# Transposing k unnormalised in the first attention, with its factors in the exps, and a new schedule for the weight rounding

## The chip, the cores and the metric

One core of a Trainium2 chip. The metric is device microseconds of one execution, checked against the reference. Engines by the names of the profile: PE does the matmuls (TensorE), DVE is VectorE, ACT ScalarE, POOL GpSimd; SP is the sync engine, in whose queue (SPq) all transfers are issued. PEclk is the granted clock: the share of full speed at which PE was allowed to run. A ratio below is the mean time of one kernel's fast runs over the mean of the fast runs of the kernel before in the same rounds on the same chip, so it is not quite the ratio of the medians quoted.

## The reference

```python
def rmsnorm(x, g):
    rms = np.sqrt(np.mean(x * x, axis=-1, keepdims=True) + 1e-06)
    return x / rms * g
q_n, k_n = rmsnorm(q, g_q), rmsnorm(k, g_k)          # q, k, v: (8, 12, 448, 64) float32
attn = softmax(q_n @ k_n.T / sqrt(64)) @ v           # for each batch and head
x = attn.transpose(0, 2, 1, 3).reshape(3584, 768)
g = np.maximum(x @ w_in, 0.0) ** 2                   # w_in (768, 2048)
return g @ w_out                                     # w_out (2048, 768)
```

The weights arrive as 64-bit floats and the kernel rounds them to 32 bits itself.

## The kernel before

Two batches form a span. For a span the kernel does the attention of twelve pairs of heads, the first product (with `w_in`) and the second (with `w_out`). Both products are done with seven block products instead of eight, so each weight becomes seven blocks: A11, A12, A22 and four sums S1 to S4. Span 0's attention runs alone; the attention of each later span is woven into the second product of the span before it.

The rounding of the weights is a pipeline of 36 ticks of four units each, woven into span 0's attention and first product. Two ticks make one pair of weight pieces and end in one write to DRAM.

```python
BLOCKS = 2                                     # two block buffers
EARLY, LATE, ALL = 4 * 13, 4 * 35, 4 * (2 * NFC + 4)   # 52, 140, 144 units
# tick t, third unit (cut)
value(t - 2, 0)                                # GpSimd, writes half of a block buffer
total(t - 3, S1, A21, A22, ALU.add)            # GpSimd
n = t - 4
if there(n) and n % 2:                         # write of a whole buffer, 1344 KB
    nc.sync.dma_start(dst.rearrange("k p m -> p k m"), blocks_of(n)[:, 0:7])
# tick t, fourth unit (cut)
nc.vector.scalar_tensor_tensor(f, low, 2.0 ** -32, high, ALU.mult, ALU.add)
value(t - 2, 1)
total(t - 3, S2, S1, A11, ALU.subtract)
total(t - 3, S3, A11, A21, ALU.subtract, nc.vector if t >= EARLY // 4 else nc.gpsimd)
total(t - 3, S4, A12, S2, ALU.subtract)
```

VectorE has four operations in a tick, ScalarE three. The products read blocks back from DRAM as `sw`, five blocks ahead, on the same sync queue that issues the writes and the loads of weight words. An instruction that waits holds up those behind it in its queue.

Span 0's normalisation multiplied q and k on GpSimd before PE's transposes; pairs 12 and later use `norm_by_squares`, whose heart is a power on GpSimd:

```python
for s in range(2):                             # q, then k
    nc.gpsimd.tensor_tensor(qkn[:, s]..., qk[:, s]..., rstd[:, s]..., ALU.mult)
...
nc.gpsimd.tensor_tensor(half, half, mhalf, ALU.pow)     # norm_by_squares, 128x28
```

## Time and profile before

| | us |
|---|---|
| median before | 1498.1 (1497.1 to 1499.4, 4 runs) |
| first product of span 0 starts (profiled run) | 154.2 |
| first scores of span 1 | 302.2 |
| second product starts | 323.6 |
| span of the profiled run | 1495.6 |

PE's matmuls are the work that sets the end; their starts in the timeline are the landmarks. After 323.6 us PE is busy 98.6% of the time, so what counts is how much PE loses before that.

### The profile page before, as it was taken

Reading aid. Unit: us, or ns where it says so; the run is one execution under the profiler, and the core shown is the slowest. Engines: PE = TensorE matmul, PEld = TensorE weight load, DVE = VectorE, ACT = ScalarE, POOL = GpSimd, SP = SyncE. Lnnn points to the kernel's source line nnn. Section 1 sums busy time; section 2 is a strip of 40 time slices with the busy share of each in tenths; the row PEclk is TensorE's granted clock in tenths of the full one; section 3 lists DMA queues with packets and bytes.
Section 4 is the critical chain, followed back from the end, with each engine's and each line's share of the span. In section 5 each row is a group of like instructions: output and inputs, shape, how many; then the busy total and the mean of one; then the engine's idle time right before and its main releaser. Section 6 shows DMA issues by size and latency. Waiting matters only on the chain.

```text
span 1495.6 us, 14182 instructions
## 1 busy us (share of the span) xinstructions
PE 1432.4 (96%) x4656; PEld 652.7 (44%) x4656; DVE 842.2 (56%) x1167; ACT 430.9 (29%) x586; POOL 571.5 (38%) x380
## 2 busy tenths in 40 slices
PE   5998898879999999999999999999999999999997
PEld 2443344424444455544444445554444445555553
DVE  2788999748776623456666643346667652332111
ACT  4786456522222201222222201122332211111000
POOL 4789888853333002444333102254333302221000
PEclk9999999989999999999999999999999999999999
DMA  6366978654444333344434442333535323233443
GB/s 185 120 200 183 282 275 303 206 152 93 99 99 99 88 101 87 92 113 87 98 86 108 89 100 86 89 101 87 109 86 116 79 70 96 85 90 100 103 116 68
DMA packets 415574, 180.37 MB, mean 121 GB/s; under 512 B 264068, under 2 KB 413444, under 8 KB 415492
## 3 DMA queue, kind: packets, MB, share of 16 engines
q1 hardware_dynamic: 415492, 179.37, 45.7%
q8 instruction: 39, 0.64, 0.2%
q14 instruction: 43, 0.35, 0.1%
HBM read 146.28 MB, written 33.03 MB: 120 GB/s over the span
## 4 chain that ended last, share of the span: by engine, by line
PE 76%; DVE 9%; POOL 6%; DMA 3%; issue 3%; ACT 2%; SPq 0%; DVEq 0%; POOLq 0%; ACTq 0%
PE ps L858 29%; PE sc L669 9%; PE pd L782 8%; PE pav L686 8%; PE pa L782 8%; PE pc L782 8%; DVE rec L703 4%; PE pb L782 4%; PE tot L697 3%; DMA sw<-w1s 2%; POOL gC L489 1%; POOL gC L482 1%; POOL rstd L612 1%; POOL qkn L614 1%; DVE qkT L647 1%
## 5 line engine op out<-in xcount | busy, mean ns | idle before, releaser
L858 PE MATMUL ps<-gT,sw 128*128 128x448 f32 x768 | 304.0, 546 | 2.6 <-DMA sw<-w2s 2.6
L634 POOL TENSOR_TENSOR half<-half,mhalf 128x28 f32<-128x28 f32 x36 | 176.8, 4911 | 320.4 <-DVE half L633 298.6
L790 POOL TENSOR_TENSOR gT<-gT 128x448 f32<-128x448 f32 x112 | 114.2, 1021 | 419.2 <-ACT gT L786 419.2
L672 ACT ACTIVATE pr<-sc 112x896 f32<-112x896 f32 x192 | 165.8, 913 | 223.8 <-PE sc L669 223.8
L858 PE MATMUL ps<-gC,sw 128*128 128x448 f32 x576 | 228.7, 545 | 0.0
L858 PEld LDWEIGHTS ps<-gT,sw 128*128 128x128 f32 x768 | 143.6, 191 | 158.6 <-issue 153.3
L669 PE MATMUL sc<-qkT 64*112 64x448 f32 x768 | 175.1, 576 | 15.1 <-ACT qkT L648 13.1
L703 DVE RECIPROCAL rec<-tot 128x448 f32<-128x448 f32 x48 | 142.0, 2958 | 70.8 <-PE tot L697 70.8
L686 PE MATMUL pav<-pr,vt 112*64 112x448 f32 x768 | 161.5, 547 | 0.8 <-DVE xT L705 0.8
L782 PE MATMUL pa<-xT,sw 128*128 128x448 f32 x384 | 155.5, 541 | 3.3 <-DMA sw<-w1s 3.3
L858 PEld LDWEIGHTS ps<-gC,sw 128*128 128x128 f32 x576 | 106.7, 190 | 117.4 <-issue 114.6
L786 ACT ACTIVATE gT<-gT 128x448 f32<-128x448 f32 x96 | 55.3, 576 | 287.9 <-DVE gT L816 174.1
L677 DVE TENSOR_TENSOR acc<-acc,pr 112x896 f32<-112x896 f32 x72 | 78.6, 1092 | 61.5 <-ACT pr L672 57.6
L669 PEld LDWEIGHTS sc<-qkT 64*112 64x112 f32 x768 | 62.4, 177 | 114.0 <-issue 67.6
L782 PEld LDWEIGHTS pa<-xT,sw 128*128 128x128 f32 x384 | 73.1, 191 | 76.4 <-issue 73.5
L648 ACT ACTIVATE qkT<-qkT,gains 128x448 f32<-128x448 f32 x36 | 24.1, 668 | 245.9 <-DVE qkT L647 245.9
L686 PEld LDWEIGHTS pav<-pr,vt 112*64 112x64 f32 x768 | 50.9, 137 | 100.7 <-issue 80.7
L677 DVE TENSOR_TENSOR acc<-pr 112x896 f32<-112x896 f32 x36 | 39.5, 1097 | 82.5 <-ACT pr L672 82.5
L782 PE MATMUL pd<-xT,sw 128*128 128x448 f32 x192 | 79.6, 551 | 5.6 <-DVE z L805 4.0
L782 PE MATMUL pd<-xC,sw 128*128 128x448 f32 x192 | 77.7, 540 | 2.8 <-DMA sw<-w1s 1.4
L782 PE MATMUL pb<-xC,sw 128*128 128x448 f32 x192 | 77.7, 540 | 2.5 <-DVE xC L722 1.8
L782 PE MATMUL pc<-xC,sw 128*128 128x448 f32 x192 | 77.5, 539 | 1.7 <-DMA sw<-w1s 1.7
(90 smaller groups left out, 1487.6 us busy)
## 6 DMA issues: line engine op xcount, KB each, us to landing
sw<-w1s SPq DMA_DIRECT2D x224, 192.0 KB, 2.4
sw<-w2s SPq DMA_DIRECT2D x168, 256.0 KB, 3.2
w1s<-gC SPq DMA_DIRECT2D x8, 1344.0 KB, 6.1
w2s<-gC SPq DMA_DIRECT2D x8, 1344.0 KB, 6.1
out_dram<-osb SPq DMA_DIRECT2D x192, 56.0 KB, 1.8
qk<-in_q_dram SPq DMA_DIRECT2D x144, 56.0 KB, 3.1
qk<-in_k_dram SPq DMA_DIRECT2D x144, 56.0 KB, 2.4
vt<-in_v_dram SPq DMA_DIRECT2D x72, 112.0 KB, 3.2
```

Source lines behind the costliest of these rows:

```text
L634: nc.gpsimd.tensor_tensor(half, half, mhalf, ALU.pow)
L648: nc.scalar.activation(qkTs[i][:, 0], qkTs[i][:, 0], AF.Copy, scale=gains[:, 0:1])
L669: nc.tensor.matmul(sc[:, h, 0:S], qkT[rows, 1, c * SP:(c + 1) * SP], qkT[rows, 0, :], start=True, stop=True)
L672: nc.scalar.activation(pr, sc[:, :, 0:S], AF.Exp)
L677: nc.vector.tensor_tensor(accs[i], probs[i, 0] if c == 1 else accs[i], pr, ALU.add)
L686: nc.tensor.matmul(pavs[i][h * D:(h + 1) * D, :], vs[i][:, h, c, :], pr[:, h, :], start=(c == 0), stop=(c == NJ - 1))
L697: nc.tensor.matmul(tots[i][h * D:(h + 1) * D, :], ones, pr[:, h, :], start=first, stop=last)
L703: nc.vector.reciprocal(rec, tots.pop(i))
L782: nc.tensor.matmul(ps, stream[n][:, c], rhs[:, c], start=first and c == 0, stop=c == HC - 1, skip_group_check=not first)
L786: nc.scalar.activation(g, src, AF.Relu)
L790: nc.gpsimd.tensor_tensor(g, g, g, ALU.mult)
L858: nc.tensor.matmul(ps, stream[n][:, c % 4], rhs_of[i][:, c], start=c == 0, stop=c == HF - 1)
```

## The change

The intent is to take work off GpSimd in span 0's attention, fit two more rounding ticks in there, and end the rounding five products before the first product ends, so that the second product finds its blocks. The core of the diff (layout of the q and k buffers and the fallback kernel are cut):

```diff
-    EARLY, LATE, ALL = 4 * 13, 4 * 35, 4 * (2 * NFC + 4)
+    EARLY, ALL = 4 * 15, 4 * (2 * NFC + 4)
...
-        total(t - 3, S3, A11, A21, ALU.subtract, nc.vector if t >= EARLY // 4 else nc.gpsimd)
+        total(t - 3, S3, A11, A21, ALU.subtract)
...
-        for s in range(2):
-            nc.gpsimd.tensor_tensor(qkn[:, s]..., ALU.mult)
+        nc.gpsimd.tensor_tensor(sq[:, 0]..., raw[:, 0]..., rstd[:, 0]..., ALU.mult)
+        normed[i] = sq[:, 0], raw[:, 1]
...
-        nc.scalar.activation(pr, sc[:, :, 0:S], AF.Exp)
+        if i < NAT:
+            for h in range(2):
+                nc.scalar.activation(pr[:, h], sc[:, h, 0:S], AF.Exp, scale=rstds[i][:, 1, 2 * c + h:2 * c + h + 1])
+        else:
+            nc.scalar.activation(pr, sc[:, :, 0:S], AF.Exp)
...
-            if span == 0 and on_scalar:
+            if span == 0:                      # all squares of span 0 on ScalarE
                 nc.scalar.activation(g, g, AF.Square)
...
-                weights(EARLY * (u + 1) // NAT)
+                weights(min(8 * (u + 1), 16 + (EARLY - 16) * (u - 1) // (NAT - 2)))
...
-                weights(EARLY + (LATE - EARLY) * (u + 1) // N1)
-    weights(ALL)
+                weights(min(ALL, EARLY + (ALL - EARLY) * (u + 1) // (N1 - 5)))
+                ahead(u, NAT)                  # norm(12) at product 35, norm(13) and load(14) at 42
```

The normalisations of pairs 12 and 13, which stood in the attention, now stand in the first product. k is loaded so that its transposes can read it as it came, in pieces of 256 B.

More of the change, by code (lines that the diff above doesn't have):

```diff
@@ L171, in softmax @@
         nc.vector.tensor_reduce(nmax, sc[:, :, 0:S], AX, ALU.max, negate=True)
-        pr = work.tile([SP, 2, S], F32, tag="pr", name="pr", bufs=3)
+        pr = work.tile([SP, 2, S], F32, tag="pr", name="pr", bufs=2)
         total = small.tile([SP, 2], F32, tag="total", name="total")
@@ L196, in values @@
                 nc.tensor.transpose(pt[:, c, :], pr[:, h, c * SP:(c + 1) * SP], ident[:SP, :SP])
-            prT = work.tile([SP, NJ, SP], F32, tag="prT", name="prT", bufs=4)
+            prT = work.tile([SP, NJ, SP], F32, tag="prT", name="prT", bufs=2)
             if h == 0:
@@ L226, in feed_forward @@
                                  start=(c == 0), stop=(c == NPAIR - 1))
-            r = work.tile([P, S], F32, tag="r", name="r")
+            r = work.tile([P, S], F32, tag="r", name="r", bufs=1)
             nc.scalar.activation(r, ph, AF.Relu)
@@ L231, in feed_forward @@
         for t in range(0, FULL + P * odd, P):
-            osb = work.tile([P, DM], F32, tag="osb", name="osb")
+            osb = work.tile([P, DM], F32, tag="osb", name="osb", bufs=1)
             for half in range(2):
@@ L301, in attention_then_ffn_with_row_max, with places_of @@
         pass
+def places_of(qk, i, work):
+    first, second = i % 2 * 4 + work, i % 2 * 4 + 2 + (i // 2 + work) % 2
+    return qk[:, first:second + 1:second - first]
 def load_pair(nc, qk, q, k, i):
@@ L307, in load_pair @@
     b, h0 = divmod(2 * i, H)
-    qk = qk[:S // 4].rearrange("p (s h e) -> p s h e", s=2, h=2)
-    for dst, src in ((qk[:, 0], q), (qk[:, 1], k)):
-        nc.sync.dma_start(dst, src[b, h0:h0 + 2].rearrange("h (p j) d -> p h (j d)", j=4))
+    qk = places_of(qk, i, 0)[:S // 4]
+    nc.sync.dma_start(qk[:, 0].rearrange("p (h e) -> p h e", h=2),
+                      q[b, h0:h0 + 2].rearrange("h (p j) d -> p h (j d)", j=4))
+    for h in range(2):
+        nc.sync.dma_start(qk[:, 1].rearrange("p (j h d) -> p j h d", j=4, h=2)[:, :, h],
+                          k[b, h0 + h].rearrange("(p j) d -> p j d", j=4))
 @with_exitstack
@@ L324, in attention_then_ffn_bounded @@
     out: bass.AP,
-    qk0,
+    qk,
 ):
@@ L385, in attention_then_ffn_bounded @@
     mhalf = consts.tile([P, 2 * (S // 32)], F32, name="mhalf")
-    qk1 = consts.tile([P, 2 * 2 * NJ * D], F32, name="qk1")
     gT = consts.tile([P, NFC, 2 * S], F32, name="gT")
@@ L484, in value, with total @@
                 nc.gpsimd.tensor_copy(dst, words_of(n).bitcast(F32)[:, part])
-        def total(n, dst, x, y, op, engine=nc.gpsimd):
+        def total(n, dst, x, y, op):
             if there(n) and n % 2:
-                b = [blocks_of(n)[:, i] for i in (dst, x, y)]
-                engine.tensor_tensor(*b, op)
+                nc.gpsimd.tensor_tensor(*[blocks_of(n)[:, i] for i in (dst, x, y)], op)
         if there(t) and doubles:
@@ L570, in attention_then_ffn_bounded @@
     pts = {}
-    qks, vs, qkTs, probs, pavs, tots, accs, normed = {}, {}, {}, {}, {}, {}, {}, {}
+    vs, qkTs, probs, pavs, tots, accs, normed, rstds = {}, {}, {}, {}, {}, {}, {}, {}
     def load(i):
-        qks[i] = (qk0, qk1)[i % 2]
         if i < NAT:
-            load_pair(nc, qks[i], q, k, i)
+            load_pair(nc, qk, q, k, i)
             return
@@ L580, in load @@
         for s, src in enumerate((q, k)):
-            dst = by_squares(qks[i])[:, s]
+            dst = by_squares(i, 0)[:, s]
             for n in range(4):
@@ L585, in load, with by_squares @@
                                   .rearrange("(g t) e -> t g e", t=32))
-    def by_squares(flat):
-        return flat[:, 0:2 * S].rearrange("p (s g e) -> p s g e", s=2, e=32)
+    def by_squares(i, work):
+        n = i % 2 * 4 + 2 * work
+        flat = qk[:, n:n + 2].rearrange("p n e -> p (n e)")[:, 0:2 * S]
+        return flat.rearrange("p (s g e) -> p s g e", s=2, e=32)
     def load_v(i):
@@ L602, in norm @@
             return norm_by_squares(i)
-        qk = qks.pop(i)[:SP].rearrange("p (s h e) -> p s h e", s=2, h=2)
-        flat_n = loads.tile([P, 4 * P * 2], F32, tag="qkn", name="qkn", bufs=2)
-        qkn = flat_n[:SP].rearrange("p (s j h d) -> p s j h d", s=2, j=NJ, h=2)
-        sq = flat_n[:SP]
-        nc.scalar.activation(sq, qk.rearrange("p s h e -> p (s h e)"), AF.Square)
-        rstd = small.tile([SP, 2, 2, NJ], F32, tag="rstd", name="rstd")
-        rflat = rstd.rearrange("p s h j -> p (s h j)")
@@ L610, in norm @@
-        nc.vector.tensor_reduce(rflat, sq.rearrange("p (n d) -> p n d", d=D), AX, ALU.add)
-        nc.vector.tensor_scalar(rflat, rflat, 1.0 / D, 1e-6, ALU.mult, ALU.add)
-        nc.gpsimd.tensor_tensor(rflat, rflat, mhalf[:SP, 0:4 * NJ], ALU.pow)
-        for s in range(2):
-            nc.gpsimd.tensor_tensor(
-                qkn[:, s].rearrange("p j h d -> p h j d"),
-                qk[:, s].rearrange("p h (j d) -> p h j d", d=D),
-                rstd[:, s].rearrange("p h j -> p h j ()").to_broadcast([SP, 2, NJ, D]),
-                ALU.mult)
@@ L619, in norm @@
-        normed[i] = qkn
+        raw, sq = (places_of(qk, i, n)[:SP] for n in range(2))
+        nc.scalar.activation(sq, raw, AF.Square)
+        rstd = rstds[i] = small.tile([SP, 2, 2 * NJ], F32, tag="rstd", name="rstd", bufs=4)
+        nc.vector.tensor_reduce(rstd, sq.rearrange("p s (n d) -> p s n d", d=D), AX, ALU.add)
+        nc.vector.tensor_scalar(rstd, rstd, 1.0 / D, 1e-6, ALU.mult, ALU.add)
+        flat = rstd.rearrange("p s n -> p (s n)")
+        nc.gpsimd.tensor_tensor(flat, flat, mhalf[:SP, 0:4 * NJ], ALU.pow)
@@ L621, in norm_by_squares @@
+        nc.gpsimd.tensor_tensor(sq[:, 0].rearrange("p (j h d) -> p h j d", j=NJ, h=2),
+                                raw[:, 0].rearrange("p (h j d) -> p h j d", j=NJ, h=2),
+                                rstd[:, 0].rearrange("p (h j) -> p h j ()", h=2).to_broadcast([SP, 2, NJ, D]),
+                                ALU.mult)
+        normed[i] = sq[:, 0], raw[:, 1]
     def norm_by_squares(i):
-        qk = by_squares(qks.pop(i))
-        qkn = by_squares(loads.tile([P, 4 * P * 2], F32, tag="qkn", name="qkn", bufs=2))
+        raw, qkn = (by_squares(i, n) for n in range(2))
@@ L624, in norm_by_squares @@
         NG = S // 32
-        nc.scalar.activation(qkn.rearrange("p s g e -> p (s g e)"), qk.rearrange("p s g e -> p (s g e)"), AF.Square)
+        nc.scalar.activation(qkn.rearrange("p s g e -> p (s g e)"), raw.rearrange("p s g e -> p (s g e)"), AF.Square)
         half = small.tile([P, 2 * NG], F32, tag="half", name="half")
@@ L636, in norm_by_squares @@
             nc.gpsimd.tensor_tensor(
-                qkn[:, s], qk[:, s],
+                qkn[:, s], raw[:, s],
                 half[:, s * NG:(s + 1) * NG].rearrange("p g -> p g ()").to_broadcast([P, NG, 32]), ALU.mult)
@@ L653, in transposes @@
                 nc.tensor.transpose(pt[:, j * SP:(j + 1) * SP],
-                                    qkn[:, s, j].rearrange("p h d -> p (h d)"), ident[:SP, :SP])
+                                    qkn[s][:, j * P:(j + 1) * P], ident[:SP, :SP])
     def take_transposes(i):
-        if i < NAT:
-            qkTs[i] = loads.tile([P, 2, S], F32, tag="qkT", name="qkT")
-            qT, kT = pts.pop(i)
-            nc.scalar.activation(qkTs[i][:, 0], qT, AF.Copy, scale=gains[:, 0:1])
-            nc.scalar.copy(qkTs[i][:, 1], kT)
+        qkTs[i] = loads.tile([P, 2, S], F32, tag="qkT", name="qkT")
+        qT, kT = pts.pop(i)
+        nc.scalar.activation(qkTs[i][:, 0], qT, AF.Copy, scale=gains[:, 0:1])
+        nc.scalar.copy(qkTs[i][:, 1], kT)
     def scores(work, i, c, pe_sums):
@@ L671, in scores @@
         pr = work.tile([SP, 2, S], F32, tag="pr", name="pr", bufs=4)
-        nc.scalar.activation(pr, sc[:, :, 0:S], AF.Exp)
+        if i < NAT:
+            for h in range(2):
+                nc.scalar.activation(pr[:, h], sc[:, h, 0:S], AF.Exp, scale=rstds[i][:, 1, 2 * c + h:2 * c + h + 1])
+        else:
+            nc.scalar.activation(pr, sc[:, :, 0:S], AF.Exp)
         probs[i, c] = pr
@@ L730, in attention @@
         for i in range(first, end):
-            if i + 3 < (NAT + 3 if alone else min(last + 2, B * NPAIR)):
+            if i + 3 < (NAT if alone else min(last + 2, B * NPAIR)):
                 load(i + 3)
@@ L734, in attention @@
             scores(work, i, 1, alone)
-            if i + 2 < (last + 2 if alone else last):
+            if i + 2 < last:
                 norm(i + 2)
@@ L747, in attention @@
             if alone:
-                take_transposes(i + 1)
+                if i + 1 < NAT:
+                    take_transposes(i + 1)
                 yield
@@ L753, in attention @@
                 combine_x(i)
-            if i + 1 == NAT or not alone and i + 1 < last:
+            if alone and i + 2 >= NAT:
+                load(i + 2)
+            if not alone and i + 1 < last:
                 transposes(i + 1)
@@ L783, in product, with activate @@
                                  stop=c == HC - 1, skip_group_check=not first)
-        def activate(g, src, on_scalar=False):
+        def activate(g, src):
             nc.scalar.activation(g, src, AF.Relu)
-            if span == 0 and on_scalar:
+            if span == 0:
                 nc.scalar.activation(g, g, AF.Square)
@@ L819, in first_product @@
             product(pa, n + A12, B21, False)
-            activate(g11, pa, True)
+            activate(g11, pa)
             yield
@@ L823, in first_product @@
             add(g21, z, pd, ALU.add)
-            activate(g21, g21, True)
+            activate(g21, g21)
             if span and f:
@@ L884, in second_product @@
         yield
-    qks[0] = qk0
     for i, g in enumerate((g_q, g_k)):
@@ L938, in attention_then_ffn_bounded @@
             if more:
-                free = 0 if span else 2
                 total, done = HC * (7 * HF + 4) - 20, 0
                 for u, _ in enumerate(attention(work, nxt, nxt + 2 * NPAIR, False)):
-                    while done < total * (u + 1 - free) // (4 * NPAIR - free):
+                    while done < total * (u + 1) // (4 * NPAIR):
                         next(rest)
@@ L973 @@
     top = bound.tile([1, 1], F32, name="top")
-    qk0 = bound.tile([128, 16 * D], F32, name="qk0")
-    load_pair(nc, qk0, q, k, 0)
+    qk = bound.tile([128, 8, 8 * D], F32, name="qk")
+    load_pair(nc, qk, q, k, 0)
     for i, g in enumerate((g_q, g_k)):
@@ L989 @@
         with tc.manual_schedule():
-            attention_then_ffn_bounded(tc, *args, qk0)
+            attention_then_ffn_bounded(tc, *args, qk)
     with small_scores.Else():
```

## The prediction

> **What bounds the kernel now.** I read the page's slices first, then a table by stage, the groups of the two first stages, and the chain at the seam between them and the rest.
>
> ```profile
> PE   5998898879999999999999999999999999999997
> DVE  2788999748776623456666643346667652332111
> POOL 4789888853333002444333102254333302221000
> ```
>
> From slice 9 on (about 330 us) the PE is at 9 tenths until the end, while VectorE and GpSimd have room. Whatever the change wins must be won in the first 325 us: span 0's attention, its first product, and the step into the second product. I cut the run at the PE's own landmarks: pair 8's first scores (105.5), first product (154.2), first scores of the next span (302.2), second product (323.6).
>
> ```profile
> core 0: us, PE busy (x) PEld busy (x) DVE busy (x) ACT busy (x) POOL busy (x), PEclk, DMA share, GB/s
> 20.00:105.50 85.50, 85.14 (x442) 34.55 (x442) 61.32 (x61) 60.94 (x79) 62.35 (x42) 1.00 0.55 169
> 105.50:154.20 48.70, 43.39 (x218) 16.90 (x217) 44.09 (x53) 31.88 (x40) 44.40 (x30) 0.96 0.68 195
> 154.20:302.20 148.00, 131.97 (x338) 63.21 (x338) 133.14 (x136) 82.93 (x116) 123.62 (x97) 0.99 0.80 268
> 302.20:323.60 21.40, 11.02 (x45) 3.49 (x44) 13.52 (x18) 7.98 (x10) 12.05 (x7) 0.76 0.62 148
> 323.60:1495.60 1172.00, 1155.59 (x3604) 532.11 (x3604) 586.22 (x889) 240.87 (x336) 319.75 (x195) 1.00 0.40 94
> ```
>
> Row 1: the attention is the PE's until pair 8. Row 3: VectorE is busy 90% and GpSimd 84%, the PE runs 338 instructions that at 0.375 us each (the chain shows 2.25 us per six) need 127 us, not 148. Row 4: half idle. Row 5 (98.6% busy) is out of the change's reach.
>
> Pair periods, from the first scores of each pair in the timeline: 10.46 us up to pair 8 (105.48), then 116.22, 127.17, 142.46, and the first product at 154.21. With 10.46 throughout, and 0.92 us less for the last pair, which transposes nothing, it would have been 146.4: **7.8 us lost**. The longest single wait there is PE's for GpSimd's q and k factors (2.5 us at 131.4); GpSimd was in a 5.4 us power just before, and two more of 5.1 us follow for pairs 12 and 13.
>
> In the first product the same instructions take longer than in the attention (here the groups of 20 to 160 us, then of 160 to 322 us):
>
> ```profile
> L493 DVE TENSOR_SCALAR gC<-words 128x768 uint32<-128x768 uint32 x6 | 3.3, 558 | 0.0
> L482 POOL TENSOR_TENSOR gC<-words,gC 128x384 f32<-128x384 f32 x10 | 10.4, 1056 | 0.0
> L489 POOL TENSOR_TENSOR gC<-gC 128x384 f32<-128x384 f32 x17 | 16.7, 1001 | 0.0
> ```
>
> ```profile
> L493 DVE TENSOR_SCALAR gC<-words 128x768 uint32<-128x768 uint32 x10 | 11.0, 1096 | 0.9 <-POOL gC L489 0.9
> L482 POOL TENSOR_TENSOR gC<-words,gC 128x384 f32<-128x384 f32 x23 | 30.7, 1346 | 4.8 <-ACT gC L502 2.1 <-ACT p L800 1.2 <-DMA w2s<-gC 0.8
> L489 POOL TENSOR_TENSOR gC<-gC 128x384 f32<-128x384 f32 x36 | 48.8, 1357 | 0.9
> ```
>
> 0.56 became 1.10, 1.0 became 1.36: in the timeline each VectorE rounding operation ends where a GpSimd one begins to advance, and the reverse. The two take turns. The seam, in the chain:
>
> ```profile
> 299.99 2.27 PE pc L782 x6
> ...
> 305.56 1.75 POOL gC L489
> 307.31 0.07 issue
> 307.38 1.01 POOL gC L489
> 308.38 1.10 issue
> 309.52 5.59 POOL half L634
> ...
> 320.32 3.24 DMA sw<-w2s
> 323.60 1.11 PE ps L858
> ```
>
> The PE finishes the product at 302.3, GpSimd the last rounding sums at 308.4; a normalisation and sixteen load issues follow on the sync queue before the first block of the second weight can be asked for.
>
> **What the Trainium skill says.** SBUF — State Buffer, "Who interferes with whom": VectorE and GpSimd share one port pair, an exclusive lock held for a whole instruction, taken by VectorE's tensor_scalar in its two-port mode and by two-SBUF-input operations against a GpSimd read; "PE and ACT never wait on anyone." The trace agrees: the doubled times above are VectorE's and GpSimd's, while ScalarE's rounding steps stay at 0.94 and 0.93 us in both stages. ScalarE: Activation LUTs, "What ACT_TABLE_LOAD costs": an activation costs 186 ns + 0.833 ns an element, a per-partition pointer adds 93 ns, neighbours overlap by 93 ns. The trace is close: 913 ns for the 896-wide exp (932 stated), 637 ns for the 448-wide copy with a gain pointer (652 stated). TensorE: Matmul & The Clock Gate, "What's actually happening": after an idle window of about 3.4 us the clock halves. Before's second product begins with 14 instructions in 7.21 us where 5.25 is normal, after the seam's idle time; the page's granted clock there is 0.76. DMA: Bandwidth & Descriptors, "Specifications": line rate needs at least 512 B; k now comes in 256 B pieces. No trace here shows that yet.
>
> **The change part by part.**
>
> *Attention, GpSimd.* Twelve k multiplications go (1.06 us each; one a pair), and the two normalisations for pairs 12 and 13 (a power of 5.1 plus two of 0.97 each: 14 us) move into the product. Two more rounding ticks come: about 11 operations of 1 us. A steady pair's GpSimd load was 3.9 + 2.1 + 1.08 ticks x 3.9 = 10.2 us, as much as the PE's 10.46; it becomes 3.9 + 1.05 + 1.1 x 3.9 = 9.2. The first two pairs take two ticks each, where GpSimd had half its time free.
> *Attention, VectorE.* A pair: reciprocal 3.0, xT 1.0, sum 1.2, factor 0.2, ticks 1.1 x 2.9 = 3.2, combinations 0.6 to 1.9: 8.6 to 10.5, no longer with 2.8 of a normalisation by squares in the last two pairs.
> *Attention, ScalarE.* Each exp of 0.82 us spacing becomes two of about 0.54 (the gain copies have 0.52): +0.26 x 48 = +12 us. Per pair 4.3 + 1.0 (square) + 1.05 (copies) + 1.1 x 2.7 = 9.3, under 10.46; the pair with two full ticks needs 11.8 and runs 1.3 late. Exp latency still fits in two score buffers, just.
> *Start.* k's own transposes no longer wait for a multiplication (about 0.3 us won); an extra issue before the gate loads costs about 0.4. Nil.
> So the pairs stay at 10.46 to the end with about 2.5 us of slips: first product at 149 instead of 154.2, **-5.2 us**.
>
> *First product.* Eight units are two ticks. Now, by spacings in the timeline, they hold four values 3.9, three sums 2.9, 1.45 squares 1.3 on GpSimd, and 5.6 + 0.5 (S3) on VectorE: 14.2 us of turns. The weight writes at 221.8 to 286.3 show five such pairs in 64.5, 12.9 each, so turns overlap by 9%. After: the squares are gone to ScalarE, S3 is back on GpSimd: 3.9 + 3.8 + 5.6 = 13.3, times 0.91 = 12.2 us. The PE needs less for the products tied to them (8 x 51 / 84 = 4.86 products x 2.25 = 10.9), so rounding stays the bound. VectorE's queue is in order, so the products' additions stand behind its rounding. Its last rounding operation is unit 132. Before, units 52 to 132 went with 51 products and took 139 us; after, 60 to 132 go with 44 products: 9 x 12.2 = 110. Add 3 us for the start (xC and z waits, 5.8 us now, less without transposes in between) and 5 for the two normalisations (four short multiplications in turns; most of each power runs beside VectorE). Then 12 products remain without VectorE rounding, less the one the PE is ahead: 11.2 x 2.25 = 25. Sum 143 to 144, against 148: **-4 us**. Most of what rounding gains is spent on twelve, not five, untied products at the PE's own pace.
>
> *Seam.* Before, 302.2 to 323.6 holds 24 score instructions x 0.21 + 20 x 0.19 = 8.9 us of work: 12.5 lost, and 2.0 more at the low clock. After, GpSimd's last sums are done about 13 us before the PE's last product, the write and first reloads need 6.1 + 3.2 us, and pair 12's and 13's transposes and normalisations lie behind the product. I leave 2 us: **-12.5 us**.
>
> Sum -21.7: 1497.8 - 21.7 = 1476.1.
>
> **Rivals.** (a) *Nothing won before the seam*: ScalarE, at 9.3 of 10.46 us a pair and in order, delays exps, and GpSimd, now with S3 and two powers, stretches the product to 150. For it: the first turns of the product took 14.3 us, not 12.9, beside weight loads. Against: GpSimd no longer waits for relus (11.3 us of idle before squares). It would give 1485 to 1488. (b) *The PE becomes the bound in the product*: if turns fall below 10.9 us, it takes 127 + 4, and with the seam the time is 1463 to 1465. Against: the same count of operations needs the lock. (c) *The transfers*: two ticks move 1.54 MB of words, 1.34 of blocks and 0.95 of sw, 3.8 MB; at the 310 GB/s seen that is 12.3 us, as long as the turns. Small pieces of pairs 12 to 14 among them could hold rounding up: 1480. (d) *The seam keeps a wait* for the last write: +5, 1481.
>
> **Range and chances.** All that can be won is 7.8 + 21 + 14.5 = 43 us (1454). The seam is nearly sure, the attention likely, the product open by 8 either way: 1476, range 1466 to 1487. Two per cent is 1467.8, which needs the product near the PE's bound: 0.14. Slower by two per cent would need a broken pipeline: 0.01.
>
> **What would show it.** First scores of the pairs 10.5 us apart to the last; first product near 149; weight writes 12.2 us apart; VectorE's rounding operations still at 1.1 us in the product; last sum well ahead of the last product; no gap over 3 us and a clock of 1.0 around the first second-product matmul. I am wrong if pair periods grow with waits on exps, if the product takes under 135 or over 150 us, or if the rest after the seam moves by more than 2 us.

## More of the kernel before

The prediction shows the lines. Two more are needed here, from the waits of 154 to 309 us (engine, line, what it waited for; total us, times, longest):

```profile
POOL gT L790 <- ACT gT L786: 11.3, 9, 3.0
...
POOL gC L482 <- DMA w2s<-gC: 3.1, 2, 2.3
```

GpSimd (POOL) waits for the relus whose squares it takes, and hardly ever for the write of a block buffer.

## The result, and the profile after

| | before | after |
|---|---|---|
| median, us | 1498.1 | 1507.6 (1504.6 to 1508.1, 4 runs) |
| first product starts (profiled run) | 154.21 | 153.65 |
| first product lasts | 148.0 | 165.4 |
| from span 1's first scores to the end | 1193.4 | 1183.8 |
| span of the profiled run | 1495.6 | 1502.8 |

The ratio is 1.0059 (1.0041 to 1.0076): slower, by less than one per cent. The differences of the profiled runs, -0.6 + 17.4 - 9.6, make the 7.2 us between their spans. The seam closed as intended; the first product lost more than it gave.

The stages of the changed kernel (columns as in the prediction's table: busy us of each engine, the granted clock, DMA share, GB/s):

```profile
0.00:153.65 153.65, 130.92 (x672) 54.38 (x673) 114.41 (x120) 113.96 (x177) 103.41 (x78) 1.00 0.70 203
153.65:319.03 165.38, 135.72 (x338) 64.91 (x336) 108.46 (x132) 87.16 (x126) 113.97 (x88) 0.95 0.71 230
```

In the first product VectorE (DVE) is now busy 66% and GpSimd 69% of the time, where they were at 90 and 84. Neither is the bound any more, and yet the stage is longer: something makes all of them wait. The waits of 150 to 330 us name it:

```profile
POOL gC L492 <- DMA w2s<-gC: 13.3, 4, 3.5
...
PE pa L793 <- DMA sw<-w1s: 8.5, 4, 4.2
...
PE pb L793 <- DMA sw<-w1s: 7.3, 1, 7.3
...
POOL gC L492 <- DMA w1s<-gC: 6.6, 2, 3.3
```

GpSimd's waits for block writes were 3.5 us (3.1 for `w2s`, 0.4 for `w1s`) and have become 19.9. PE waits for blocks (`sw`) whose loads stand in the sync queue behind those writes: 21.7 us in this product, against 9.3 before. PE's own busy time grew as well, from 131.95 to 135.72 us, at the lower granted clock of 0.95. The two together are 16 of the 17.4 us. One turn of the loop, from the chain that ended last (start, duration, what):

```profile
230.75 6.07 DMA w2s<-gC
...
236.97 1.02 POOL gC L492
237.99 0.95 POOL gC L498
238.94 1.70 POOL gC L492
240.64 1.34 POOL gC L498 x2
...
243.56 1.32 POOL gC L498
244.90 6.11 DMA w2s<-gC
```

The write of a buffer takes 6.1 us; only then may GpSimd put the first value (L492) into that buffer, and two values and four sums (L498) follow before the next write can be issued: 14.15 us from write to write. The chain goes round this loop with no other engine in it, apart from the turns that stretch some sums. The writes before and after, from the sync queue's timeline:

```profile
247.48 0.37 SPq L519 DMA_DIRECT2D w2s<-gC  x1
260.52 0.37 SPq L519 DMA_DIRECT2D w2s<-gC  x1
273.27 0.37 SPq L519 DMA_DIRECT2D w2s<-gC  x1
286.29 0.37 SPq L519 DMA_DIRECT2D w2s<-gC  x1
```

```profile
244.90 0.37 SPq L528 DMA_DIRECT2D w2s<-gC  x1
258.06 0.37 SPq L528 DMA_DIRECT2D w2s<-gC  x1
275.08 0.37 SPq L528 DMA_DIRECT2D w2s<-gC  x1
296.04 0.37 SPq L528 DMA_DIRECT2D w2s<-gC  x1
302.01 0.37 SPq L528 DMA_DIRECT2D w2s<-gC  x1
```

Before, 13 us apart. After, 13.2, then 17.0 and 21.0: the two normalisations. In the second of them GpSimd first stands idle for 5.5 us (278.0 to 283.5), because its power comes next in the queue and must wait for ScalarE's square (280.1) and VectorE's sums (done at 283.4). What PE makes of the last one, in the chain:

```profile
283.52 4.79 POOL half L639
...
296.04 0.37 SPq L528
...
296.50 6.16 DMA sw<-w1s
...
302.80 4.82 PE pb L793 x6
```

The power delays the sums, they delay the write, the loads of PE's next blocks stand behind that write, and PE is idle for 7.3 us; its first six matmuls then take 4.8 us instead of 2.3, at a granted clock of 0.50.

The attention won nothing. From pair 2 to pair 3 it takes 13.2 us instead of 10.46 (scores at 42.61 and 55.78), and the last two pairs take 11.7 and 12.8. The first of the two, in the timeline:

```profile
134.60 4.22 DVE L730 TENSOR_TENSOR xC<-xT,xC 128x448 f32<-128x448 f32 x1
135.42 2.92 POOL L498 TENSOR_TENSOR gC<-gC 128x384 f32<-128x384 f32 x3
140.92 0.94 ACT L505 ACTIVATE words<-words 128x768 f32<-128x768 f32 x1 [4.86 <-DVE words L532]
144.74 2.06 PE L673 MATMUL sc<-qkT 64*112 64x448 f32 x8 [2.15 <-ACT pr L678]
```

An operation of 0.62 us takes 4.22 and ends half a microsecond after GpSimd's run of sums (138.3); ScalarE's rounding step waits for VectorE, pair 11's exps stand behind it in ScalarE's queue, and PE waits for a score buffer.

This profiled run is the fastest of the four, and it flatters the attention. Five profiled runs have the same attention code (this one and four experiments below: squares on GpSimd, normalisations late, load late, cheap power). In two of them pair 3 takes 13.0 and 13.2 us and the first product starts at 151.5 and 153.7. In the other three PE waits 3.0 to 3.1 us instead of 2.2 for the buffer in pair 3, its granted clock over the matmuls that follow is 0.68 to 0.80 instead of 1.00, pair 3 takes 16.0 to 17.1 us, and the product starts at 156.8 to 159.3. So a wait that is a little longer goes with 3 to 4 us more in these runs. Read the experiments on the product by its length too, and not by the time alone.

Landing times answer a question that the prediction left open: k's loads in pieces of 256 B took 3.5 us for 112 KB from issue to landing (median, 20 to 130 us), against 3.7 us for 224 KB before. No wait of PE or ScalarE for them shows in the attention.

### The profile page after: what moved, and what is told of

Same layout as the page of the kernel before. It is cut to its first block, busy times and chain, and to the rows that moved or that the text cites. A ratio compares the mean times of both kernels' runs of the same rounds, so it can differ in the third digit from the quotient of the medians.

```text
span 1502.8 us, 14259 instructions
## 1 busy us (share of the span) xinstructions
PE 1430.3 (95%) x4656; PEld 653.6 (43%) x4656; DVE 821.6 (55%) x1156; ACT 450.7 (30%) x650; POOL 543.8 (36%) x363
## 4 chain that ended last, share of the span: by engine, by line
PE 76%; DVE 10%; POOL 4%; DMA 4%; issue 3%; ACT 2%; SPq 0%; POOLq 0%; DVEq 0%; ACTq 0%
PE ps L869 27%; PE sc L673 10%; PE pav L694 9%; PE pd L793 8%; PE pc L793 8%; PE pa L793 7%; DVE rec L711 5%; PE pb L793 4%; PE tot L705 3%; POOL gC L498 2%; DMA sw<-w1s 1%; DMA w2s<-gC 1%; POOL gC L492 1%; ACT qkT L653 1%; DVE qkT L652 1%
## 5 line engine op out<-in xcount | busy, mean ns | idle before, releaser
L801 POOL TENSOR_TENSOR gT<-gT 128x448 f32<-128x448 f32 x96 | 94.9, 990 | 405.1 <-ACT gT L797 405.1
L680 ACT ACTIVATE pr<-sc 112x896 f32<-112x896 f32 x144 | 124.3, 914 | 191.7 <-PE sc L673 191.6
L793 PE MATMUL pa<-xT,sw 128*128 128x448 f32 x384 | 156.8, 545 | 8.5 <-DMA sw<-w1s 8.5
```

What stands on the lines that cost most here:

```text
L680: nc.scalar.activation(pr, sc[:, :, 0:S], AF.Exp)
L793: nc.tensor.matmul(ps, stream[n][:, c], rhs[:, c], start=first and c == 0, stop=c == HC - 1, skip_group_check=not first)
L801: nc.gpsimd.tensor_tensor(g, g, g, ALU.mult)
```

## The experiments

Theory W: the block buffer's write, which GpSimd's shorter and denser queue no longer hides, sets the pace of the rounding in the product, and the two powers stretch it twice (the normalisations of pairs 12 and 13). Rival L, the prediction's own: turns at the port that VectorE and GpSimd share set the pace, so what counts is the sum of their operations. All edits are to the changed kernel unless said otherwise.

**S3 back on VectorE.**

```diff
-        total(t - 3, S3, A11, A21, ALU.subtract)
+        total(t - 3, S3, A11, A21, ALU.subtract, nc.vector if t >= 13 else nc.gpsimd)
```

> The changed kernel with the eleven S3 differences back on VectorE. Theory W (write loop): two block buffers; the next pair's first value waits for the 6.1 us write of the buffer, then six GpSimd operations follow before the next write, so the period of the weight writes is 6.1 + 6 x 1.3 = 14, and one operation less on GpSimd takes 1.0 to 1.3 us off each of about 8 periods: 8 to 10 us faster than the changed kernel, near 1498. Theory L (turns at the shared port, as predicted): S3 takes 0.97 on GpSimd and 0.5 on VectorE, so 0.5 a period: 4 us faster, near 1503.

Measured: 1503.3 (1499.6 to 1507.9), ratio 1.0047. About 4 us by the medians, 2 by the ratios: nearer to rival L's number than to W's, but the intervals overlap (1.0025 to 1.0069, against 1.0041 to 1.0076 for the changed kernel), so nothing at all is not excluded. The waits on block writes stayed (21 us). W overrated what one operation less in the loop is worth.

**Squares of g22 and g12 back on GpSimd.**

```diff
-            if span == 0:
+            if span == 0 and on_scalar:        # True for g11 and g21 only
```

> The changed kernel with the sixteen squares of g22 and g12 back on GpSimd. Theory W: they fit into the time in which GpSimd waits for the write, so nothing to 4 us slower (1507 to 1511). Theory L: 16 more operations of 0.9 us take turns with VectorE: 12 to 14 us slower (1519 to 1521).

Measured: 1507.9, ratio 1.0061 against 1.0059: nothing. Sixteen operations more on GpSimd cost no time, and its waits for block writes fell from 19.9 to 11.2 us. This is W's result; under L they would have cost 12 us.

**The write cut in two.** A11, A12 and A22 go out as soon as the values are there, S1 to S4 after the sums.

```diff
-            nc.sync.dma_start(dst.rearrange("k p m -> p k m"), blocks_of(n)[:, 0:7])
+            for i, j in ((S2, A12), (S4, S4 + 1)):
+                nc.sync.dma_start(dst[i:j].rearrange("k p m -> p k m"), blocks_of(n)[:, i:j])
...
         value(t - 2, 1)
+        if there(t - 2) and (t - 2) % 2:       # dst, m: as for n, with m = t - 2
+            for i, j in ((A11, S2), (A12, S4)):
+                nc.sync.dma_start(dst[i:j].rearrange("k p m -> p k m"), blocks_of(m)[:, i:j])
```

> The changed kernel with each block write cut in two: A11, A12 and A22 go out as soon as the values are there, S1 to S4 after the sums, so that the next pair's values wait for no write that was only just issued. Theory W: the 6.1 us write falls out of the loop; waits of GpSimd on the block writes (20 us in the first product) vanish, periods fall from 14.2 to about 12.2 (then the port's turns bind): 12 to 16 us faster, 1491 to 1495. Theory L: the waits only shift, within 3 us of 1507.

Measured: 1497.5, ratio 0.9995 (0.9977 to 1.0013): 10 us off. GpSimd's waits on block writes are gone from the product (first product 158.9 us, against 165.4); one of 6.9 us on a `w1s` write is left just before it. The periods from 190.66 to 253.84 are 12.6 us on average; the uncut kernel has 13.6 over the same writes (190.15 to 258.06). The loop is shown, a little smaller than expected, and the two long periods are still there (18.6 and 22.8). The cut also makes the second write shorter, so that the loads behind it in the sync queue can land sooner; a third block buffer, which would part the two effects, was not tried.

**The normalisations behind the rounding.**

```diff
-                ahead(u, NAT)
+                if u == 50: norm(NAT)
+                if u == 52: norm(NAT + 1); load(NAT + 2)
+                if u == 54: transposes(NAT)
```

> The changed kernel with the two normalisations by squares and the load of pair 14 moved behind the last rounding (products 50 and 52 instead of 35 and 42). If they cost the two long write periods (17.0 and 21.0 against 14.2) and the 7 us wait of PE on the last blocks, 8 to 10 us come back, less a new gap at the seam of up to 5: 1500 to 1504, with periods of 13 to 14.5 throughout. If they cost only the 5 us predicted: 1503 to 1506.

Measured: 1494.6 (1491.0 to 1498.9), ratio 0.9989: 13 us off by the medians, 10 to 11 by the ratios, at or above the top of what was expected. The first product takes 154.0 us, 11.4 less. The periods at the end are 13.9, 13.3 and 13.1; PE waits 1.7 us for span 1's first scores, so the seam stays closed.

**Only the load of pair 14 moved** to product 52.

> The changed kernel with only the load of pair 14 moved behind the rounding (product 52); the two normalisations stay at 35 and 42. If eight load issues of 6 us on the sync queue held the blocks up, 5 us or more come back of the 13 that the late normalisations won. If it is GpSimd's powers standing in front of the sums and so of the block writes, at most 2: 1505 to 1508, the periods of 17 and 21 us stay.

Measured: 1507.4, ratio 1.0056: nothing; the long periods are still 19.8 and 21.0. The eight load issues in the sync queue are not the cause.

**A multiplication in place of the two powers** (wrong result).

```diff
-        nc.gpsimd.tensor_tensor(half, half, mhalf, ALU.pow)
+        nc.gpsimd.tensor_tensor(half, half, mhalf, ALU.mult if i in (NAT, NAT + 1) else ALU.pow)
```

> Wrong result on purpose: the changed kernel with the power of pairs 12 and 13 replaced by a multiplication of the same operands (0.1 to 0.2 us instead of 5). If the power's 5 us in front of the sums in GpSimd's queue make the write periods of 17 and 21 us, they fall to 14 to 16 and 8 to 11 us come back: 1497 to 1500. If the rest of the normalisation (ScalarE's square, VectorE's sum, two multiplications) does it: 1504 to 1507.

Measured: 1498.3 (1493.6 to 1502.7), ratio 0.9987: 9 us off. The power's length is a good part of what the late normalisations won; how much stays open. By time this run and that one can't be told apart (intervals 0.9964 to 1.0011 and 0.9966 to 1.0012). But the first product takes 160.2 us here, between 165.4 and 154.0, and the periods are still 17.9 and 16.5: GpSimd stands 4.1 and 3.8 us before the two short multiplications, waiting for VectorE's sums of the normalisation. So by the traces about half is the power, and the waiting in the queue is the likely rest. These six results settle the product: the write loop, and the two normalisations in GpSimd's queue.

**Both repairs.**

> The changed kernel with both repairs: block writes cut in two and the normalisations behind the rounding. The first alone took 10 us off, the second 13. If they act on different waits (the write loop, and GpSimd's powers between the sums), they add: 22 us off the changed kernel, 1485, periods of 12.6 to the end, first product of 142 to 146 us. If both only relieved the same late loads of PE: 14 to 16 us off, 1491 to 1493.

Measured: 1481.1 (1477.7 to 1482.3), ratio 0.9886 (0.9869 to 0.9903). They add, and even a little more than that: 26 us off the changed kernel, 17 off the kernel before. The first product:

```profile
153.14:294.18 141.04, 130.59 (x338) 62.35 (x336) 116.83 (x133) 86.61 (x127) 118.84 (x86) 1.00 0.80 263
```

141 us, VectorE and GpSimd busy 83 and 84%, the clock full. The second parts of the writes come 12.5 us apart (160.75 to 260.82 in eight periods), close to the 12.2 that the prediction worked out from turns at the port. They are as close to the 12.3 of its rival (c), the transfers: over these periods the transfers ran at 301 GB/s, DMA share 0.86. Which of the two binds here is not shown. This version beats both kernels.

**Both repairs and S3 on VectorE.**

> Both repairs (1481) and S3 on VectorE. With the write out of the loop the periods are 12.5 us, near the 12.2 worked out for the turns at the port. If the turns bind now, S3 there saves 0.5 us a period: 3 to 5 us sooner, 1476 to 1478. If GpSimd's own queue binds, 1.0 a period: 1472 to 1474. If something else does (words, the PE), nothing.

Measured: 1486.8, ratio 0.9924: 5.5 us slower than without, against the expectation of both theories. The waits of 154 to 300 us:

```profile
POOL gC L492 <- ACT gT L505: 16.5, 3, 10.7
POOL gC L492 <- ACT gC L505: 11.4, 3, 4.6
POOL gC L492 <- ACT words L505: 9.1, 7, 3.1
...
PE pd L800 <- DVE gT L834: 6.8, 4, 2.3
```

GpSimd now waits 37 us for ScalarE's step L505, which follows VectorE's last rounding operation (no such wait shows without S3 on VectorE), and PE for VectorE's additions. S3 takes 1.29 us on VectorE here, turns included, and VectorE's queue is in order. Counting turns alone had left that queue out. With both repairs in place, S3 is better on GpSimd.

**The kernel before with its writes cut in two.**

> The kernel before with only its block writes cut in two. If the wait for the write was made by the change (before, squares and a shorter run of sums hid it: its GpSimd waited 3.5 us on block writes in all), nothing to 4 us are won: 1494 to 1498. If the loop bound the kernel before as well, 8 to 12 us: 1486 to 1490.

Measured: 1496.9, ratio 0.9990 (0.9977 to 1.0004). The write did not bind the kernel before. The change itself turned it into the bound.

**Rounding spread evenly over the attention.**

```diff
-                weights(min(8 * (u + 1), 16 + (EARLY - 16) * (u - 1) // (NAT - 2)))
+                weights(EARLY * (u + 1) // NAT)
```

> The changed kernel with the fifteen ticks spread evenly over the attention (five units a pair) instead of two whole ticks in each of the first two pairs. If the front load delays pair 3 (13.2 us from pair 2 to pair 3, against 10.5), that pair comes back to 10.5 and the first product starts 2 to 3 us sooner: 1504. If the delay there is from pieces of k or from the two exps per head, pair 3 stays late: 1507.

Measured: 1509.3, ratio 1.0079. Pair 3 came back to 10.5 us (42.47 to 52.96), so the front load is what delays it. But later pairs lost more: PE waits 4.3 us for exps in pair 11, and the first product starts at 156.96. The expected whole was wrong, the expected detail right.

**No rounding beside pairs 10 and 11** (13 ticks in the attention, all before).

> The changed kernel with thirteen ticks in the attention, all before pair 10, and none beside pairs 10 and 11. If rounding beside the last combinations makes the last two pairs late (11.7 and 12.8 us, against 10.5 and 9.5: VectorE's xC waits behind GpSimd's sums, ScalarE's rounding step behind VectorE, the exps behind that), they fall to 10.5 to 11 and 9.5 to 10.5, 3 to 4 us sooner, while the whole is no faster because two ticks more fall into the product (plus 10). If it is the exps themselves, they stay.

Measured once, state unknown: 1508.9. The last two pairs took 11.5 and 10.5 instead of 11.7 and 12.8, the first product began at 150.3. Rounding beside them costs 2.5 us, mostly in pair 11. Pair 10 stays late for another reason; its xC still takes 5.6 us beside a run of GpSimd's sums.

**One exp for both heads** (wrong result).

> Wrong result on purpose: one exp for both heads with the first head's factor, as wide as before the change. It takes 12 us of ScalarE's work out of the attention. If the split exps delay PE, pair 3 or the last two pairs become shorter by 1 to 3 us; if ScalarE is only late because its rounding step waits for VectorE, the pair distances stay within 0.5 us.

Measured once, state unknown: 1508.2. The last pairs take 11.4 and 12.8 us, pair 3 is late again. The exps' own length is not the cause.

**k normalised again, on both repairs.** A first form wrote the normalised k into the place where a later load puts raw k, ahead of the transposes:

> Both repairs, but k normalised by GpSimd before its transposes again, and one exp for both heads: the headline of the change undone. If a pair's GpSimd load of 10.2 against 9.2 us matters beside 15 ticks, pairs slip, first product at 156 to 159 instead of 153, 1484 to 1487. If it was never what held the pairs, the time stays within 2 us of 1481.

Measured: 1521.9 and a wrong result. The edit was at fault, and the run says nothing on its question, only why the change keeps k where it was loaded. The second form multiplies in place:

```diff
+        nc.gpsimd.tensor_tensor(kn, kn, rstd[:, 1]..., ALU.mult)     # kn is raw[:, 1]
-            for h in range(2):
-                nc.scalar.activation(pr[:, h], ..., AF.Exp, scale=...)
+        nc.scalar.activation(pr, sc[:, :, 0:S], AF.Exp)
```

> Both repairs, with k normalised on GpSimd in place before its transposes and one exp for both heads, the right result this time. If GpSimd's load of a pair (10.2 against 9.2 us, by the prediction) holds pairs beside 15 ticks, several pairs take over 10.5 us and the first product starts 3 to 6 us later than 153: 1484 to 1487. If pair distances are set elsewhere (front load, last pairs), within 2 us of 1481.

Measured: 1483.6, correct, ratio 0.9898 against 0.9886: k's factors in the exps are worth about 2 us. The intervals overlap (0.9882 to 0.9915, 0.9869 to 0.9903), so it may be nothing. Apart from pair 3, pairs take 10.5 us up to pair 8 with the multiplication as without. The first product starts at 156.7, 3.6 us later than in the run without; pair 3 (14.3 us against 13.2) and the last two pairs (12.5 and 13.8 against 11.8 and 12.8) make the difference, which lies within the spread of starts named above.

## Why the prediction was wrong

The forecast was 1476, a gain of 21.7; the kernel lost 9.5. By its own steps:

- **What bounds the kernel before** held. PE after 325 us, an end of about 43 us to win, and VectorE's in-order queue as the tie between rounding and products: the run of the kernel before with cut writes confirms that the write did not bind there.
- **Attention, -5.2 us**: measured -0.6 in the profiled runs. The step "the pairs stay at 10.46 to the end with about 2.5 us of slips" failed: the slips were about 7, 2.7 at pair 3 and 4.5 in the last two pairs. The front load was checked on GpSimd and ScalarE; the trace shows VectorE late: its rounding stood in front of the reciprocal at 45.58, and PE waited 2.2 us for the buffer that the following multiplication frees. In the last pairs VectorE was counted by its durations, without the time that it waits for GpSimd and without the exps queued behind a rounding step. GpSimd's load of a pair, from which the gain was derived, is worth about 2 us, or nothing, by the run that puts k's multiplication back. The exps themselves were sized right: ScalarE: Activation LUTs, "What ACT_TABLE_LOAD costs", gives 0.56 us spacing for 448 elements with a pointer as scale, and four in a row took 2.21 us.
- **First product, -4 us**: measured +17.4. This is the step that decided. Its sentence "they hold four values 3.9, three sums 2.9 ... so turns overlap by 9%. After: ... 13.3, times 0.91 = 12.2 us" took a period that agreed with one limit for proof of that limit. It looked at the operations between two writes and not at what the first of them waits for: two block buffers and a write of 6.1 us, a time that stood in the page. Removing squares made GpSimd free in the very time in which it had to wait. With the write cut and the normalisations moved away, 12.5 and 141 us were measured against 12.2 and 143 to 144. That agreement is again no proof that turns bind there: rival (c)'s 12.3 fits as well, and taking turns away (S3 on VectorE, both repairs) made the kernel slower. The overlap of 9% was also taken from the last five periods; all nine before average 13.5 us, not 12.9.
- **"5 for the two normalisations (... most of each power runs beside VectorE)"**: measured 10 to 13. It is true that VectorE goes on beside the power, but the sums behind it in GpSimd's queue do not. They wait for the power and also for the square and the sums that come before it, and write, block loads and PE hang on the sums.
- **Seam, -12.5 us**: -9.6. Right in kind: no gap, the second product 1.7 us after span 1's first scores. The term was some 3 us too large.
- **Rivals**: (a) came nearest in kind, a product stretched, with GpSimd's powers as part of it, but gave 150 us and 1485 to 1488. None named GpSimd's wait for the write of a block buffer inside the product ((d) named the last write, at the seam). The range held only if the product stayed under 155.

Open: how much of the 1 us that pair 10 still loses is VectorE's wait for GpSimd; which limit sets the 12.5 us; and what makes the wait in pair 3 2.2 us in one run and 3.0 in the next. The profiled runs show the start of the first product anywhere from 151 to 159 us with the same code in the attention; that wait and the lower clock after it make 3 to 4 us of this, and some 3 us are there before (first scores of pair 2 at 40.5 to 43.8). That this is why the changed kernel's times spread over 3.5 us and some of its relatives over 8, where the kernel before keeps within 2.3 in its four runs, is likely but not shown: only one run of each kernel has a trace.

## What to carry to other kernels

A measured period that agrees with one limit does not exclude a second just below it: for every buffer in a loop, add up its own round trip, write included, before taking work out from beside it. Work that an engine does during a wait can be free: here sixteen operations put back on GpSimd cost nothing. A long instruction in an in-order queue costs what hangs on the instructions behind it, so it belongs where nothing does; cutting a write so that its early parts leave early was worth 10 us here, and placing two normalisations late 10 to 13.

## What the Trainium skill lacked or had wrong

- SBUF — State Buffer, "Who interferes with whom": the lock and which operations take it agree with this case. It says that whoever issues first gets the pair for one instruction; it does not say who is next. Here a VectorE subtraction of 0.62 us with two SBUF inputs took 4.22, 5.63 and 6.14 us in three kernels, each time ending about 0.5 us after the last of four to six GpSimd operations that stood back to back, while in the first product the same operation took 1.31 us and the two engines alternate. What decides between the two is open.
- No page gives the length of GpSimd's power: 112x16 took 2.9 to 5.4 us and 128x28 took 4.8 to 5.6, against 0.24 us for a multiplication of the same 128x28 (the cheap power's run) and 1.0 us for one of 128x384. What makes one power longer than another of its size is open.
